# Attention and a residual MLP in one kernel: the first batch's attention in groups of four heads, mixing in column halves, PSUM in three pools, and the first MLP block by quarters of a weight

## The chip, the cores and the metric

The kernel runs on one core of one Trainium2 chip. The metric is the device time of one execution in microseconds, as the median of many runs. Engines are called as in the profile: PE is the matrix engine, PEld its weight loads, DVE the vector engine, ACT the scalar engine, POOL the GpSimd engine, and SP the engine that here only issues transfers.

## The reference, cut to what matters

```
q, k, v: (8 batches, 8 heads, 576 positions, 64)   float32
k_p, v_p = means of k, v over 8 positions each      -> 72 pooled positions
attn  = softmax(0.125 * q @ k_p^T)                  -> 576 x 72 for each head
x     = attn @ v_p, heads side by side              -> (8, 576, 512)

a1    = alpha1 * x + beta1
tok   = w_tok @ a1                                  (mixes the 576 positions of a batch)
u     = x + lam * tok
a2    = alpha2 * u + beta2
out   = u + lam * (relu(a2 @ w_ch1) @ w_ch2)        w_ch1: 512 x 2048, w_ch2: 2048 x 512
```

## The kernel before

**Tiles.** The 576 positions of a batch are four chunks of 128 and a rest of 64. Two batches put their rests together, so that two batches make nine chunks; all 36 chunks are worked through by the MLP in nine blocks of four chunks (`NBLK`). Block 0 holds chunks 0 to 3 of batch 0, block 1 those of batch 1, block 2 begins with the joint rest of batches 0 and 1.

**Attention of a batch.** `att_F` transposes q (on PE for batches 0 and 1, by a transposing transfer later), `att_Frem` the rest. `sum_k` (on POOL) and `att_K` pool k; batch 0 has no `sum_k`, and there `double_k` copies a slice instead. `att_V` pools v by three adds on DVE (batch 0: `first_V`, on PE). The scores come from `att_S4` for four heads at once: two banks `hi`, two banks `lo` and two for the rests, and twelve exponentials on ACT in two groups of six. Batch 0 uses `att_S` instead, head by head, with keys padded by zeros in `kpT_pool`. `att_AV` multiplies by v and divides on DVE (L524, L526) into `x_tm`; `att_X` and `rest_X` multiply by lam and alpha1 into `xs`.

**Mixing and MLP.** `mix_T` multiplies a chunk by w_tok (five products of 512 columns; the fifth brings the last 64 positions, beta1 and the row sums that `setup_rowsum` makes), adds x into `u_sb` and makes `u_bf = u * alpha2`. `mix_uT` brings it feature-major into `u_fm`: for block 0 by PE transposes and an ACT copy, for all others by a transposing transfer on SP's queue. `mlp_A(n, j)` makes hidden rows j of block n (j from 0 to 15) with a relu on ACT; `mlp_B(n, m, part)` multiplies them by a quarter of w_ch2 for chunk m, and after part 3 DVE scales and adds (L649, L650) and SP stores.

**PSUM.** Eight banks: `psA` has six, handed out in turn by `gp(name)`, `psB` two (tag "ch": fillers, `lo`, and `mlp_B` for chunks 0 and 1). A bank is given out again when its readers are through.

**Order.** The schedule is written by hand. Every engine executes its instructions in program order. First a straight list (L659 to L748) does batch 0's attention, its mixing, and the first four `mlp_A` in column halves, with `keep_warm` fillers for PE. Then each block n is a list of (position, action) that is sorted by position: `mlp_A` j at j, `mlp_B` at 16 + 4m + part, and in between the attention and mixing of batch n + 1 and the loads for batch n + 2. In block 0 `att_K(1, 1)` stands at 8.6, `att_S4(1, 0)` at 9.0, `att_S4(1, 1)` at 13.6 and the mixing of batch 1 from 21.0 on. A transfer waits in its queue; POOL's queue is also POOL's instruction stream, so a load is issued only when the work before it on POOL is done.

Of the kernel before, what the change touches and what calls it, by code (L numbers as in the profile page):

```python
# [23 lines left out]
def kernel(  # L24
# [24 lines left out]
    psA = ctx.enter_context(tc.tile_pool(name="psA", bufs=6, space=bass.MemoryType.PSUM))  # L49
    psB = ctx.enter_context(tc.tile_pool(name="psB", bufs=2, space=bass.MemoryType.PSUM))  # L50

    def gp(name):
        return psA.tile([P, 512], FP, tag="gp", name=name)

# [115 lines left out]
    def load_wtok():  # L170
# [4 lines left out]
        nc.gpsimd.dma_start(out=wt_bf[0:REM, 4 * S:5 * S], in_=moe_w_tok[512:576, :])  # L175

# [3 lines left out]
    b2row = const.tile([4, P], FP, tag="b2row", name="b2row")  # L180
# [18 lines left out]
    nc.scalar.dma_start(out=b2row, in_=moe_beta2.rearrange("(c p) -> c p", p=P))  # L199
# [32 lines left out]
    vp1_pool, kpT_pool, kp_pool, ET_pool = [], [], [], []  # L232
    for i in range(4):
# [3 lines left out]
        if i < 2:  # L237
            t = const.tile([P, 2, 4, SPG], BF, tag=f"kpT_{i}", name=f"kpT_{i}")
            nc.vector.memset(t, 0.0)
            kpT_pool.append(t)  # L240
            kp_pool.append(const.tile([P, 4, SPG], BF, tag=f"kp_{i}", name=f"kp_{i}"))
# [14 lines left out]
    def bias_row(i):  # L256
        p0 = 64 - 64 * i
        nc.vector.tensor_tensor(out=xs_pool[i][p0:p0 + 1, 4, :], in0=vecs[p0:p0 + 1, 1],
                                in1=vecs[p0:p0 + 1, 0], op=ALU.mult)

    b2c_bf = const.tile([P, 4], BF, tag="b2c_bf", name="b2c_bf")
    wtT = const.tile([P, 6, 640], BF, tag="wtT", name="wtT")
# [8 lines left out]
    def load_al2(behind):  # L271
        behind.memset(al2_bc[:, 0:1], 0.0)
        nc.sync.dma_start(out=al2_bc, in_=moe_alpha2.unsqueeze(0).to_broadcast((P, DM)))

    def spread_lam():

        ps = gp("ps_bc")
# [3 lines left out]
    def spread_al1(half):  # L281

        ps = gp("ps_bc")[:, 0:256]
# [4 lines left out]
    def setup_vectors():  # L288
        ps = gp("ps_vec")
        nc.tensor.transpose(out=ps[:, 0:4], in_=b2row, identity=identity[0:4, 0:4])  # L290
        nc.scalar.copy(out=b2c_bf, in_=ps[:, 0:4])

    def setup_wtok(tcx, copy):
# [4 lines left out]
        ps_w = gp("ps_w").bitcast(BF)  # L298
# [7 lines left out]
    def setup_rowsum(tcx):  # L306
# [3 lines left out]
        ps = gp("ps_rs")  # L310
# [32 lines left out]
    def setup_bias(g):  # L343
        ps_bias = gp("ps_bias")
# [8 lines left out]
    def att_F(b, hp, copy=nc.scalar.copy):  # L353
# [11 lines left out]
        ps_q = gp("ps_q").bitcast(BF)  # L365
# [30 lines left out]
    def att_K(b, u, copy):  # L396
# [21 lines left out]
        for a in range(2):  # L418
# [442 lines left out]
```

The softmax here doesn't subtract the row's maximum and nothing guards it: scores larger than these inputs give would overflow.

## Time and profile before

| what | value |
|---|---|
| median of 13 runs | 346.08 us (345.45 to 349.08) |
| the profiled execution itself | 348.03 us, span 346.3 us |
| busy in the span | PE 334.8, PEld 177.1, DVE 224.7, ACT 146.9, POOL 91.3 us |
| moved by DMA | 45.77 MB, mean 132 GB/s |
| `mlp_A` products (L609), `mlp_B` products (L643) | 132.1 us, 128.5 us |
| mixing products (L572) | 44.8 us |
| PE begins block 1 | 71.62 us |
| PE begins blocks 2 and 3 | 107.21 and 143.70 us |

A matmul of 512 columns takes 216 ns in a row of them; its own record reads about 379 ns, since its end is modelled and overlaps the next. Busy sums are averages over the whole span. The first 72 us differ from the rest: there all weights and the data of three batches are loaded, at 122 to 273 GB/s in the first eight of the forty slices.

### The profile page before, as it was taken

Reading aid. Unit: us, or ns where it says so; the run is one execution under the profiler, and the core shown is the slowest. Engines: PE = TensorE matmul, PEld = TensorE weight load, DVE = VectorE, ACT = ScalarE, POOL = GpSimd, SP = SyncE. Lnnn points to the kernel's source line nnn. Section 1 sums busy time; section 2 is a strip of 40 time slices with the busy share of each in tenths; the row PEclk is TensorE's granted clock in tenths of the full one; section 3 lists DMA queues with packets and bytes.
Section 4 is the critical chain, followed back from the end, with each engine's and each line's share of the span. In section 5 each row is a group of like instructions: output and inputs, shape, how many; then the busy total and the mean of one; then the engine's idle time right before and its main releaser. Section 6 shows DMA issues by size and latency. Waiting matters only on the chain.

```text
span 346.3 us, 5862 instructions
## 1 busy us (share of the span) xinstructions
PE 334.8 (97%) x2181; PEld 177.1 (51%) x2221; DVE 224.7 (65%) x476; ACT 146.9 (42%) x277; POOL 91.3 (26%) x105
## 2 busy tenths in 40 slices
PE   8999999979999999999999999999999999999995
PEld 3667654445544554455445544554455445545544
DVE  6674578787676668875867598758685882037511
ACT  3656980048303840286018700890079005704700
POOL 8768603601126011801180027001600100000000
PEclk9999999999999999999999999999999999999999
DMA  8999999987758925896379628991810132011012
GB/s 122 191 221 273 213 205 220 166 158 130 157 182 186 189 45 136 195 209 80 104 211 188 98 75 207 180 157 53 227 62 1 39 84 78 0 61 62 2 50 71
DMA packets 66654, 45.77 MB, mean 132 GB/s; under 512 B 34457, under 2 KB 57373, under 8 KB 66626
## 3 DMA queue, kind: packets, MB, share of 16 engines
q1 hardware_dynamic: 51716, 32.73, 41.3%
q0 software_dynamic: 14448, 12.40, 22.6%
q8 instruction: 17, 0.28, 0.3%
q10 hardware_dynamic: 462, 0.27, 0.3%
q14 instruction: 11, 0.09, 0.1%
HBM read 38.30 MB, written 9.44 MB: 138 GB/s over the span
## 4 chain that ended last, share of the span: by engine, by line
PE 82%; DMA 12%; POOL 2%; DVE 1%; issue 1%; SPq 0%; ACT 0%; DVEq 0%; POOLq 0%
PE ps_h L609 31%; PE ps_ch L643 31%; PE ps_tok L572 9%; DMA u_fm<-u_bf 5%; DMA w<-in_moe_w_ch_dram 4%; DMA rem_raw<-in_k_dram 3%; PE ps_av L518 2%; PE ps_s L474 2%; PE ps_ch L632 1%; PE ps_warm L563 1%; PE ps_kp L404 1%; POOL k_raw L162 1%; POOL k_bf L164 1%; PE ps_sc L454 1%; PE ps_bc L278 1%
## 5 line engine op out<-in xcount | busy, mean ns | idle before, releaser
L614 ACT ACTIVATE Hj<-ps_h,bias_cols 128x512 bf16<-128x512 f32 x144 | 98.3, 689 | 167.3 <-PE ps_h L609 166.0
L609 PE MATMUL ps_h<-u_fm,w 128*128 128x512 bf16 (+1 forms) x572 | 132.1, 374 | 3.3 <-DMA u_fm<-u_bf 2.0
L643 PE MATMUL ps_ch<-w,Hj 128*128 128x512 bf16 x543 | 128.5, 379 | 1.2 <-issue 0.5
L609 PEld LDWEIGHTS <-w 128*128 128x128 bf16 x592 | 63.7, 114 | 54.1 <-issue 5.7
L643 PEld LDWEIGHTS <-Hj 128*128 128x128 bf16 x560 | 52.9, 98 | 62.1 <-issue 2.1
L572 PE MATMUL ps_tok<-xs,wtT 128*128 128x512 bf16 (+2 forms) x199 | 44.8, 380 | 0.6 <-DVE xs L540 0.3
L649 DVE TENSOR_TENSOR ps_ch<-lam_bc,ps_ch 128x512 f32<-128x512 f32 x32 | 22.2, 693 | 32.8 <-PE ps_ch L643 32.5
L540 POOL TENSOR_TENSOR xs<-x_tm,lamal_bc 128x512 bf16<-128x512 f32 x10 | 12.7, 1268 | 111.2 <-DVE x_tm L526 109.5
L576 DVE TENSOR_TENSOR u_sb<-x_tm,ps_tok 128x512 f32<-128x512 f32 (+1 forms) x40 | 27.4, 684 | 10.9 <-PE ps_tok L572 10.7
L524 DVE RECIPROCAL rec<-ps_av 128x5 f32<-128x5 f32 x64 | 12.2, 191 | 32.5 <-PE ps_av L522 32.4
L526 DVE TENSOR_TENSOR x_tm<-ps_av,rec 128x320 f32<-128x320 f32 x64 | 31.5, 492 | 2.7
L650 DVE TENSOR_TENSOR u_sb<-u_sb,ps_ch 128x512 f32<-128x512 f32 x35 | 24.0, 687 | 13.6 <-PE ps_ch L643 12.5
L503 ACT ACTIVATE ET<-ps_s 72x512 f16<-72x512 f32 x56 | 32.3, 592 | 0.0
L442 DVE TENSOR_TENSOR v_u<-v_u 72x512 f32<-72x512 f32 (+1 forms) x56 | 30.9, 551 | 1.0
L579 DVE TENSOR_TENSOR u_bf<-u_sb,al_bc 128x512 bf16<-128x512 f32 x34 | 26.9, 792 | 3.5 <-DMA u_fm<-u_bf 2.4
L572 PEld LDWEIGHTS <-wtT 128*128 128x128 bf16 (+3 forms) x200 | 17.3, 100 | 21.3 <-issue 1.7
L162 POOL TENSOR_TENSOR k_raw<-k_raw 128x512 f32<-128x512 f32 x14 | 18.4, 1314 | 12.5 <-DMA k_raw<-in_k_dram 12.5
L164 POOL TENSOR_TENSOR k_bf<-k_raw 128x512 bf16<-128x512 f32 x14 | 18.4, 1317 | 1.1
L518 PEld LDWEIGHTS <-ET 72*128 72x128 f16 x256 | 14.1, 97 | 8.7 <-DVE vp L435 0.2
L79 POOL DMA_DIRECT2D q_bf<-in_q_dram x16 | 12.6, 788 | 14.6 <-DVE v_u L136 13.3
L540 DVE TENSOR_TENSOR xs<-x_tm,lamal_bc 128x512 bf16<-128x512 f32 x22 | 15.4, 702 | 0.7
L518 PE MATMUL ps_av<-vp,ET 72*128 72x66 f16 x256 | 15.8, 193 | 0.2 <-issue 0.2
(121 smaller groups left out, 214.6 us busy)
## 6 DMA issues: line engine op xcount, KB each, us to landing
out_dram<-u_sb SPq DMA_DIRECT2D x32, 256.0 KB
k_raw<-in_k_dram SPq DMA_DIRECT2D x12, 512.0 KB
v_u<-in_v_dram SPq DMA_DIRECT2D x12, 512.0 KB
q_bf<-in_q_dram POOLq DMA_DIRECT2D x16, 256.0 KB, 6.4
w<-in_moe_w_ch_dram POOLq DMA_DIRECT2D x8, 512.0 KB, 15.1
v_u<-in_v_dram POOLq DMA_DIRECT2D x2, 576.0 KB, 16.5
k_raw<-in_k_dram POOLq DMA_DIRECT2D x2, 512.0 KB, 15.5
rem_raw<-in_q_dram SPq DMA_DIRECT2D x15, 64.0 KB
```

Of the source, the lines that this page charges most:

```text
L442: nc.vector.tensor_tensor(out=t[:, :, 0:n], in0=t[:, :, 0:n], in1=t[:, :, n:2 * n], op=ALU.add)
L503: nc.scalar.activation(out=o, in_=i, func=AF.Exp, bias=0.0, scale=0.125)
L518: nc.tensor.matmul(out=av[:, odd + c, :], lhsT=ET[:, m0:m0 + 128], rhs=vp1[:, hh, :])
L526: nc.vector.tensor_tensor(out=x[:, 1 - odd:6 - odd, dd:dd + D], in0=av[:, :, 0:64], in1=rec.unsqueeze(2).to_broadcast((P, 5, D)), op=ALU.mult)
L540: eng.tensor_tensor(out=xs[:, 0:4, cols], in0=x[:, 1:5, cols], in1=lamal_bc[:, cols].unsqueeze(1).to_broadcast((P, 4, D * (h1 - h0))), op= ...
L572: nc.tensor.matmul(out=ps_tok[p0:p1], lhsT=wtT[0:kk, at, P * c:P * c + p1 - p0], rhs=xs_pool[i][0:kk, sc, :], start=(sc == 0), stop=(sc == 4))
L576: nc.vector.tensor_tensor(out=s["u"][p0:p1, :], in0=x[p0:p1, 1 + c if c < 4 else 5 - 5 * i, :], in1=ps_tok[p0:p1, 0:DM], op=ALU.add)
L579: eng.tensor_tensor(out=s["u_bf"], in0=s["u"], in1=al2_bc, op=ALU.mult)
L609: nc.tensor.matmul(out=ps_h[:, t0:t1], lhsT=w1_of(cc, j), rhs=u_fm[n][:, cc, t0:t1], start=(cc == 0), stop=(cc == 3))
L614: nc.scalar.activation(out=t, in_=ps_h, func=AF.Relu, bias=bias_cols[:, j:j + 1], scale=1.0)
L643: nc.tensor.matmul(out=ps, lhsT=Hj[n, j][:, 128 * m:128 * m + 128], rhs=w2[j // 4][:, j % 4, :], start=(j == 0), stop=(j == NJ - 1))
L650: nc.vector.tensor_tensor(out=u, in0=u, in1=ps, op=ALU.add)
```

## The change

- Batch 0 takes its scores by `att_S4` too; `att_S` and `kpT_pool` go. The list of the front is put in a new order: heads 2 and 3 first, `setup_vectors` earlier, twelve fillers instead of sixteen.
- Mixing of batch 0 is done in column halves: `mix_half` multiplies by the first four row groups for 256 columns (four heads), and `mix_T` adds the fifth product at the end.
- Chunks 1 and 3 of block 0 have no `u_bf`: `mix_uT_fp` transposes `u_sb` itself in fp32 and multiplies by alpha2, held as columns in `al2c`, on the way out of PSUM.
- Batch 1's chunks are transposed on PE, as batch 0's were, and no longer by a transfer.
- PSUM: `psA` four banks, `psB` two, and a new `psX` with two (`xp`), which takes `hi`, heads 2 and 3 of `att_AV`, `mlp_B` for chunks 2 and 3, and work of the front.
- Block 0 does parts 0 and 1 of `mlp_B` for all four chunks, then parts 2 and 3 chunk by chunk.
- Loads: alpha2's rows go to POOL's queue in the front; batch 1's k is issued after batch 0's last `att_X`; batch 1's v in two halves, each after a quarter of w_ch1, and all of these after the mixing's `u_bf` products. In block 0 some positions move (`att_V`, heads 0 to 3 of `att_AV`, mixing 21.5 instead of 21.0).

```diff
-    psA = ctx.enter_context(tc.tile_pool(name="psA", bufs=6, space=bass.MemoryType.PSUM))
+    psA = ctx.enter_context(tc.tile_pool(name="psA", bufs=4, space=bass.MemoryType.PSUM))
     psB = ctx.enter_context(tc.tile_pool(name="psB", bufs=2, space=bass.MemoryType.PSUM))
+    psX = ctx.enter_context(tc.tile_pool(name="psX", bufs=2, space=bass.MemoryType.PSUM))
+    def bp(name):
+        return psB.tile([P, 512], FP, tag="ch", name=name)
+    def xp(name):
+        return psX.tile([P, 512], FP, tag="hi", name=name)
...
# load_wtok
+        nc.gpsimd.dma_start(out=al2_bc, in_=moe_alpha2.unsqueeze(0).to_broadcast((P, DM)))
...
-    nc.scalar.dma_start(out=b2row, in_=moe_beta2.rearrange("(c p) -> c p", p=P))
+    nc.scalar.dma_start(out=b2row[0:4], in_=moe_beta2.rearrange("(c p) -> c p", p=P))
+    nc.scalar.dma_start(out=b2row[4:8], in_=moe_alpha2.rearrange("(c p) -> c p", p=P))
...
# setup_vectors
-        nc.tensor.transpose(out=ps[:, 0:4], in_=b2row, identity=identity[0:4, 0:4])
+        nc.tensor.transpose(out=ps[:, 0:8], in_=b2row, identity=identity[0:8, 0:8])
         nc.scalar.copy(out=b2c_bf, in_=ps[:, 0:4])
+        nc.scalar.copy(out=al2c, in_=ps[:, 4:8])
...
# att_K, batch 0
-        for a in range(2):
-            rows = slice(64 * a, 64 * a + 64)
-            (copy or (nc.scalar.copy, nc.vector.tensor_copy)[a])(
-                out=kpT_pool[u][rows, a], in_=kp[rows])
+        for i, eng in ((2, nc.scalar.copy), (0, nc.scalar.copy if u else nc.vector.tensor_copy)):
+            eng(out=kp_pool[u][:, i:i + 2], in_=kp[:, i:i + 2])
...
# att_S4
-        lo = [psB.tile([P, DM], FP, tag="ch", bufs=2, name="ps_s") for _ in range(2)]
-        hi = [gp("ps_s") for _ in range(2)]
-        r = [gp("ps_r")[0:SPG, 0:128].rearrange("p (h i) -> p h i", i=64) for _ in range(2)]
+        lo = [(bp if b else gp)("ps_s") for _ in range(2)]
+        hi = [xp("ps_s") for _ in range(2)]
+        r = [(gp if b else bp)("ps_r")[0:SPG, 0:128].rearrange("p (h i) -> p h i", i=64)
+             for _ in range(2)]
...
# att_AV
-        ps_av = gp("ps_av")
+        ps_av = (xp if b and h in (2, 3) else gp)("ps_av")
...
+    def mix_half(c, half):
+        if half == 0:
+            ps_mix[c] = gp("ps_tok")
+        cols = slice(256 * half, 256 * half + 256)
+        for sc in range(4):
+            nc.tensor.matmul(out=ps_mix[c][:, cols], lhsT=wtT[:, sc, P * c:P * c + P],
+                             rhs=xs_pool[0][:, sc, cols], start=(sc + half == 0), stop=False)
...
# mix_T
-        for sc in range(5):
+        first = b == 0 and c < 4
+        ps_tok = ps_mix[c] if first else gp("ps_tok")
+        for sc in range(4 if first else 0, 5):
...
+        if eng is not None:
+            eng.tensor_tensor(out=s["u_bf"], in0=s["u"], in1=al2_bc, op=ALU.mult)
+
+    def mix_uT_fp(c):
+        ps = xp("ps_uT")
+        if 0 not in u_fm:
+            u_fm[0] = work.tile([P, 4, 512], BF, tag="u_fm", bufs=3, name="u_fm")
+        for cc in range(4):
+            nc.tensor.transpose(out=ps[:, 128 * cc:128 * cc + 128],
+                                in_=st2[0, c]["u"][:, 128 * cc:128 * cc + 128], identity=identity)
+        for cc in range(4):
+            nc.vector.tensor_scalar(out=u_fm[0][:, cc, 128 * c:128 * c + 128],
+                                    in0=ps[:, 128 * cc:128 * cc + 128],
+                                    scalar1=al2c[:, cc:cc + 1], scalar2=None, op0=ALU.mult)
...
# mix_uT
-        if blk:
+        if key[0] > 1 or key == (0, 4):
             nc.sync.dma_start_transpose(out=u_fm[blk][:, :, 128 * at:128 * at + 128],
...
# the list of the front, as it is after the change
+    load_q_bf(1, 0)
+    bias_row(0, nc.gpsimd)
+    load_q_bf(1, 1)
...
+    att_Frem(0, nc.scalar.copy)
+    setup_vectors()
+    keep_warm(1)
+    double_k(0)
+    att_K(0, 0, None)
+    keep_warm(1)
+    def scores(u):
+        att_S4(0, u)
+        for k in range(6):
+            st1[0]["exp", u](k)
+    scores(0)
+    double_k(1)
+    first_V(0, 0)
+    att_K(0, 1, None)
+    att_AV(0, 2)
+    att_F(0, 2, bank=xp)
+    att_F(0, 3, nc.vector.tensor_copy, xp)
+    att_AV(0, 3)
+    spread_al1(0)
+    att_X(0, 2, 4, nc.gpsimd, False)
+    att_AV(0, 0)
+    keep_warm(1)
+    scores(1)
+    first_V(0, 1)
+    att_AV(0, 1)
+    att_X(0, 0, 2, nc.gpsimd, False)
+    rest_X(0, 0, 4, nc.gpsimd)
+    keep_warm(1)
+    att_AV(0, 4)
+    spread_al1(1)
+    att_AV(0, 5)
+    load_rem(1, behind=nc.vector)
+    att_X(0, 4, 6, nc.gpsimd, False)
+    keep_warm(1)
+    setup_wtok(0, nc.scalar.copy, xp)
+    setup_wtok(1, nc.scalar.copy, xp)
+    att_AV(0, 6)
+    att_AV(0, 7)
+    att_X(0, 6, 8, rest=False)
+    rest_X(0, 4, 8)
+    for u in range(2):
+        load_k(1, u, queue=nc.gpsimd)
+    setup_wtok(2, nc.scalar.copy, bp)
+    setup_wtok(3, nc.scalar.copy, bp)
+    mix_half(0, 0)
+    setup_rowsum(0)
+    mix_half(1, 0)
+    setup_rowsum(1)
+    mix_half(2, 0)
+    mix_half(0, 1)
+    setup_rowsum(2)
+    mix_T(0, 0, nc.gpsimd)
+    mix_half(3, 0)
+    setup_rowsum(3)
+    mix_half(1, 1)
+    mix_T(0, 1, None)
+    mix_half(2, 1)
+    mix_T(0, 2, nc.gpsimd)
+    mix_half(3, 1)
+    mix_T(0, 3, None)
+    load_w1(2)
+    load_v(1, 0, (2,), queue=nc.gpsimd)
+    load_w1(3)
+    load_v(1, 1, (2,), queue=nc.gpsimd)
+    for g in range(2):
+        load_w2(g)
+    setup_bias(0, bp)
+    mix_uT_fp(1)
+    mix_uT((0, 0))
+    setup_wtok(4, nc.scalar.copy, bp)
+    setup_bias(1, bp)
+    mlp_A(0, 0, 0, 256)
+    mix_uT((0, 2))
+    mix_uT_fp(3)
+    for j in range(1, 4):
+        mlp_A(0, j, 0, 256)
+    for j in range(4):
+        mlp_A(0, j, 256, 512)
...
# attention(b): positions in block 0
-            at = 26.6 if first else 25.5
+            at = 27.5 if first else 25.5
...
-            for i, dt in enumerate((2.9, 3.4, 4.6, 5.1) if u else (5.7, 6.2, 2.9, 3.4)):
+            late = ((5.7, 6.2, 4.0, 4.5), (2.9, 3.4, 4.6, 5.1))[u]
+            for i, dt in enumerate(late if first else (2.9, 3.4, 4.6, 5.1) if u else (5.7, 6.2, 2.9, 3.4)):
...
-            todo.append(((6.6, 8.7, 10.0, 12.6)[i] if first else 0.2 + 2.0 * hp, lambda hp=hp: att_V(b, hp)))
+            todo.append(((9.5, 9.6, 11.6, 11.7)[i] if first else 0.2 + 2.0 * hp, lambda hp=hp: att_V(b, hp)))
...
-            at = 21.0 + 1.3 * c
+            at = (21.5 if first else 21.0) + 1.3 * c
...
-                todo.append((at + 1.8, lambda key=key: mix_uT(key)))
+                todo.append((at + (2.6 if first and c < 4 else 1.8), lambda key=key: mix_uT(key)))
...
# the blocks
-                at = 16 + 4 * m + part
+                at = 16 + (4 * part + m if n == 0 and part < 2 else 4 * m + part)
+                if n == 0 and part > 1:
+                    at = 24 + 2 * m + part - 2
...
-                    at = (14.51 if b == 1 else 21.0) + 0.01 * u
+                    at = (15.01 if b == 1 else 21.0) + 0.01 * u
```

## The prediction

> **What bounds the kernel now.** I read the page first: PE is busy for 334.8 of 346.3 us, so a change pays only where it removes PE work from the end-setting order or closes a PE gap. Next the chain of waits, for where it leaves PE:
>
> ```profile
> 22.36 9.08 DMA rem_raw<-in_k_dram
> ...
> 38.00 14.76 DMA w<-in_moe_w_ch_dram
> 52.80 2.75 PE ps_ch L643 x12
> ...
> 58.11 13.37 DMA u_fm<-u_bf x2
> 71.62 4.48 PE ps_h L609 x20
> ```
>
> Up to 71.6 us the chain runs through transfers, afterwards almost only through PE. Block 1 begins at 71.62; everything behind it (274.7 us) is PE in a fixed order. So I ask one thing: when does block 1 begin? The PE timeline gives its gaps, 0.24, 0.34 and 1.81 us:
>
> ```profile
> 31.78 1.91 PE L609 MATMUL ps_h<-u_fm,w 128*128 128x256 bf16 x16 [0.24 <-ACT u_fm L595]
> ...
> 47.03 1.06 PE L609 MATMUL ps_h<-u_fm,w 128*128 128x512 bf16 x4
> ...
> 52.80 2.75 PE L643 MATMUL ps_ch<-w,Hj 128*128 128x512 bf16 x12 [0.34 <-DMA w<-in_moe_w_ch_dram]
> ...
> 71.62 3.62 PE L609 MATMUL ps_h<-u_fm,w 128*128 128x512 bf16 x16 [1.81 <-DMA u_fm<-u_bf]
> ```
>
> The reader is to see that only the last one is worth a change of its own.
>
> The table of stretches shows DMA occupied without a break (a share over 1 in every stretch from 20 to 66 us). How long POOL's loads then take from issue, the views by line and by tile tell; first w_ch1's last quarter (issued at 26.2), then v_u, batch 1's v in two halves (issued at 22.5 and 23.2):
>
> ```profile
> DMA to landing us min/median/max: 16.7/16.7/16.7
> ```
> ```profile
> L139 POOL DMA_DIRECT2D v_u<-in_v_dram x2: 728/741/754, 22.5 to 23.2; - x2
> ...
> DMA to landing us min/median/max: 15.2/16.5/17.8
> ```
>
> So v_u's halves land at 22.5+15.2=37.7 and 23.2+17.8=41.0, w_ch1's last quarter at 26.2+16.7=42.9. This is a queue worked off in order: what is put ahead arrives first, what is put behind arrives later. Last the timeline of DVE, for three rows that the sum needs: the att_X that ends the front, two of the three adds of an att_V, and a u_bf product beside POOL's sum_k, which takes 1.62 where 0.69 is usual:
>
> ```profile
> 22.08 0.69 DVE L540 TENSOR_TENSOR xs<-x_tm,lamal_bc 128x512 bf16<-128x512 f32 x1
> ...
> 41.80 1.14 DVE L442 TENSOR_TENSOR v_u<-v_u 72x512 f32<-72x512 f32 x2
> ...
> 61.99 1.62 DVE L579 TENSOR_TENSOR u_bf<-u_sb,al_bc 128x512 bf16<-128x512 f32 x1
> ```
>
> **The front (to the fifth mlp_A).** Scores: 16 ACT exps (0.70 a head, 5.6) become 12 (as in block 0: 0.44 for two, then 0.49 each, 4.8); PE 8x0.30 becomes 2x0.72, -0.96; four fillers go, -0.86. kpT's memsets (-0.6 DVE, early) and half-row copies (0.39/0.46) become 144-column copies (0.27/0.31 by their slope). k16's second half lands at 6.06+5.8=11.9 as now, and double_k(1) now stands ahead of first_V on DVE: ready 12.15. From 13.1 (att_K 0.72 and an AV on PE first) DVE has eight AVs x0.70, a qT copy and two alpha1 products x0.41, 0.49, 0.06 and att_X 0.69: 8.1, done at 21.2 against 22.75. DVE, not PE, sets this stage: take DVE's cover away and the PE savings above would show; as it is they only lengthen PE's waits. Halves cost no extra columns (eight of 0.108 and a tail of 0.216 against five of 0.216), and more weight loads hide, as under mlp_A's 256-column halves now (16 in 1.74 us). PE has by then three column halves of mixing (3x0.43) behind it. From 21.2: the other five halves 2.16, four tails 0.86, two row sums 0.56, to 24.85; two bias groups 1.10, a bf16 transpose 0.22, wtok 0.28, fp32 transposes 0.53, to 27.0; then mlp_A 3.46, 0.22, 0.53: 31.35 instead of 33.52, **2.2 earlier**. Two u_bf (1.38) and two ACT copies (1.18) become eight DVE products (about 0.25 each from the 72x128 row's 0.29, 2.0), the first four under bias and wtok, the last under mlp_A. bias_row moves from DVE (0.68) to POOL, whose wait for k16 covers it (0.5 idle plus 0.9); rest_X is halved (0.43 DVE, 0.87 POOL); al2c's copy is 0.15 ACT; the second b2row load costs 0.25 of ACT's queue, and setup_vectors at 7.9 waits for it (bounds 0 and 1 us: its twin was issued at 3.96; I take 0, since k16 lands only at 8.1 anyway).
>
> *The fp32 transposes.* No 128x128 one is in the trace. The nearest fp32 rows are b2row's transpose (weight load 133 ns, one pass) and the broadcast product (0.62 for 256 columns in two passes). The first gives 4x0.133=0.53 a chunk, the second 1.24. [...] I take 0.53; the other end costs 1.4 more, and is covered as shown below.
>
> **Loads and queues.** al2_bc goes from SP to POOL's queue ahead of w_ch1 (0.57 of POOL); same bytes, landed by 25 both ways. The two k_raw leave 13.8/15.5 for about 20.7, behind att_X on POOL; the queue holds work to 28.2 then, so they still land near 29.4 and 30.8. w_ch1(2) to w_ch2(1) now stand behind both u_bf products on POOL: u_bf done at 26.4, six issues 4.2, 30.6; cast_rem 1.1, sum_k 2.6, an issue 0.58, sum_k 2.55: k_bf(1) at 37.5 against 38.0. PE, 2.2 early, wants it at 37.5: no wait. And v_u's second half now follows w_ch1(3): it lands at 42.9, not 41.0. SP's queue loses al2_bc (0.35) and four u_fm transposes (1.2 to 2.0 each), which brings batch 2's qT transposes forward, not back. Batch 2's k, v and rem loads go from position 14.5 to 15.0: their seven gating memsets (0.6 of DVE) come behind AV 0's evacuation, at about 49.4 instead of 48.4; sum_k(2) then ends near 68 instead of 67, and PE asks for it at 75: nothing.
>
> **Block 0, first half.** That is the cost. DVE executes att_V(2), att_V(3) at 42.9 or later (2x1.38), and only then AV 2 and 3 (0.70+0.63): 47.03. Those AVs now take psX's two banks, which att_S4(1,1) needs for hi. PE would be there at about 44.4 and stands for some 2.5 us; after it 0.06, 0.11+0.08+0.22: att_S4 ends at **47.45, before it was 47.03**. So the 2.2 of the front is spent, with 0.4 more. The same slack takes in the fp32 bound (+1.4, u_fm later) and waits on gp, four banks instead of six, while ACT lags by up to 1.1 us on a stretch where it is busy 4.5 of 5 us (bounds 0 and 0.8). [...]
>
> **Block 0, second half.** From the fifteenth mlp_A to the block's end it was 69.81-47.03=22.78. The order by quarters needs w_ch2's third and last quarter at positions 24 and 25, about 58 us, against landings of 50.3 and 52.8: -0.34. Four PE transposes of batch 1's u: +0.88, with ACT copies on an idle ACT. The gap of 1.81 goes, since u_fm no longer queues behind batch 2's k and v. Late next is DVE: all four output evacuations (1.39 each) fall into the last 8 us, with 1.4 a chunk for u. By my sum chunk 3's u_bf is ready 2.2 us before its transpose and DVE ends 1.5 us after PE; three u_bf beside POOL's sum_k at +0.93 would be 2.8 more. That is covered until batch 2's kp copy (PE wants it 6.5 us into block 1; I get 4.6 to 7.3): bounds 0 and 0.8, taken 0, the case without overlap being the nearer row (two of five u_bf overlapped before).
>
> Block 1 begins at 47.45+22.44+0.88=70.77 instead of 71.62: **-0.85**. Later blocks: mlp_A 7 reuses the bank of mlp_A 6, whose relu ends at 150.88 where PE comes at 150.93; taken 0, bounds 0 and 0.1 a block. The gap of 0.22 at block 2 stays. The profiled execution (346.3 span, 1.73 around it, 348.03, which is 1.95 above the median of 13) would be 345.45 and 347.2; the median 346.08-0.85=**345.2**.
>
> **Rivals.**
> *A, the sum above (0.42).* Its own range is 344.4 to 346.0, for a landing 0.8 us either way. 0.3% of the time is 1.04 us, about what a measurement of this kernel can tell from no change; A straddles it, half and half.
> *B, the front's gain survives (0.32).* If v_u's second half lands by 41.4, DVE is the limit: 41.4+2.76+1.33+0.42=45.9, block 1 at 69.2: -2.4, 343.7. For it: v_u's 0.59 MB took 3.3 to 3.6 us where w_ch1(3) behind it took only 1.9, so the two overlap in the queue, and one may slip past the other. Against: the order of landing was so far the order of issue.
> *C, the load queue runs dry (0.21), slower.* w_ch1(2) used to be issued at 21.7; it now waits for the second u_bf. k_raw is through at 30.8, and the shortest issue to landing in this trace is 4.8 us, of it about 3.5 latency, so from an issue at 27.3 on every microsecond is one of idle DMA and one later for v_u, att_S4(1,1) and the end. I have 26.4: a margin of 0.9. At 29.8 (the front gains nothing and loses 0.8) v_u lands at 45.4, block 1 begins at 73.3: 347.7. For it: the front is a long sum. Against: DVE's stretch is nearly gapless and made of measured rows.
> *D, the closed gap comes back (0.05).* If DVE lags, PE stands at chunk 3's transpose for what DMA cost before (-0.93 lost): 346.1.
>
> Faster: B and half of A, 0.52; same: half of A and D, 0.27; slower: C, 0.21. The range 343.2 to 347.6 reaches to B and C at their worked prices and leaves out about 0.1 on each side: B with a stage that runs under its sum, C with an issue after 29.8 or with the dearer ends of the unknown costs added to it.
>
> **What would show it.** Right: mlp_A's fifth near 31.4; PE waiting 2 to 3 us at ps_s near 45 for DVE's x_tm, DVE before it for v_u; no wait for w or u_fm in block 0; block 1 at 70.8. An fp32 transpose row near 0.13 and not 0.3. Wrong: no wait at that ps_s (B), w_ch1(2) issued after 28 (C), or PE waiting on kp or ps_uT behind DVE near 68 to 76.

## The result, and the profile after

The changed kernel takes **349.99 us** (median of 11 runs, 347.48 to 355.95) against 346.27 for the kernel before in the same comparison: ratio 1.0096, 95% interval 1.0077 to 1.0115, so 1% slower. Forecast were 345.2 and a range of 343.2 to 347.6. Ratios compare only executions that lie within 1.5% of the fastest of their kernel; the medians quoted are of more executions, so that a few long ones can lift a median above what its ratio says.

The profiled execution took 348.22 us with a span of 346.5. First its PE timeline in the places where the prediction had put something. Columns: start, duration, engine, line, operation, shapes, count, and in brackets the idle time before and what ended it.

```profile
9.28 0.24 PE L293 MATMUL ps_vec<-identity,b2row 8*128 8x8 f32 x1 [0.75 <-DMA b2row<-in_moe_alpha_dram]
9.46 0.61 PE L554 MATMUL ps_warm<-warm 128*128 128x512 bf16 x1
...
12.58 1.07 PE L432 MATMUL ps_v<-v,pool_v 128*72 128x256 f16 x4
...
27.98 0.63 PE L591 MATMUL ps_uT<-identity,u_sb 128*128 128x128 f32 x4
28.45 0.39 PE L610 MATMUL ps_uT<-identity_bf,u_bf 128*128 128x128 bf16 x4
...
33.76 0.65 PE L371 MATMUL ps_q<-identity_bf,q_bf 128*128 128x128 bf16 x8
34.61 1.03 PE L626 MATMUL ps_h<-u_fm,w 128*128 128x512 bf16 x3 [0.20 <-ACT Hj L631]
...
47.91 0.30 PE L461 MATMUL ps_s<-qT,kp 64*72 64x256 bf16 x1 [0.33 <-DVE x_tm L517]
...
48.53 0.30 PE L461 MATMUL ps_s<-qT,kp 64*72 64x256 bf16 x1 [0.33 <-DVE x_tm L517]
...
71.96 2.32 PE L626 MATMUL ps_h<-u_fm,w 128*128 128x512 bf16 x10
```

The reader is to see five things. PE waits 0.75 us for the second row load of b2row, a place that had no wait before. The filler behind it takes 0.61 us, where the fillers at 18.87 and 20.18 of the same profile take 0.38; the four products of first_V take 1.07, where those of its second call, at 17.81, take 0.63. Four fp32 transposes begin 0.47 us ahead of the next group: 0.12 each. The front's first four mlp_A are through at 33.76, where PE turns to q's transposes, and the fifth begins at 34.61, not near 31.4. Block 1 begins at 71.96 without a wait for u_fm, but it is not earlier.

At ps_s, near 48, PE waits only 0.33 us twice, since it comes there late itself. DVE, too, is late there by PE's lateness: it copies kp when PE has done att_K(1,1), and only then starts the four att_V, which run without a gap up to the evacuations that free psX:

```profile
41.07 0.46 DVE L420 CAST kp<-ps_kp 128x288 bf16<-128x288 f32 x1 [2.15 <-PE ps_kp L414]
```

In the chain of waits, which in the kernel before ran here through PE and the copies out of PSUM, now stands the new load:

```profile
4.24 4.79 DMA b2row<-in_moe_alpha_dram
```

It is issued at 4.24 on ACT's queue and is there at 4.24+4.79=9.03. Last the table of stretches. Its columns: the stretch and its length, busy time and count of PE, PEld, DVE, ACT and POOL, then the granted clock, the DMA share and GB/s.

```profile
28.00:30.00 2.00, 2.00 (x37) 1.83 (x35) 1.46 (x5) 1.23 (x4) 2.00 (x3) 1.00 0.59 198
30.00:32.00 2.00, 2.00 (x22) 1.99 (x21) 1.09 (x5) 0.59 (x1) 2.00 (x3) 1.00 0.73 92
32.00:34.00 2.00, 2.00 (x22) 1.99 (x21) 0.63 (x2) 1.29 (x3) 2.00 (x5) 1.00 1.24 214
```

DMA is less than fully busy from 28 to 32 (a share of 0.59 and 0.73), since POOL issues w_ch1(2) only at 28.98. This is the picture of rival C; whether it is also the price had to be tried.

### The profile page after: what moved, and what is told of

Its sections match the earlier page's. It is cut to its first block, busy times and chain, and to the rows that moved or that the text cites. A ratio compares the mean times of both kernels' runs of the same rounds, so it can differ in the third digit from the quotient of the medians.

```text
span 346.5 us, 5909 instructions
## 1 busy us (share of the span) xinstructions
PE 336.2 (97%) x2210; PEld 179.5 (52%) x2249; DVE 222.9 (64%) x477; ACT 147.2 (42%) x277; POOL 92.9 (27%) x108
## 4 chain that ended last, share of the span: by engine, by line
PE 90%; DVE 4%; ACT 2%; DMA 1%; issue 1%; ACTq 1%; DVEq 0%
PE ps_ch L660 34%; PE ps_h L626 33%; PE ps_tok L575 11%; PE ps_s L461 2%; PE ps_av L509 2%; DVE v_u L444 2%; DMA b2row<-in_moe_alpha_dram 1%; ACT Hj L631 1%; PE ps_tok L564 1%; PE ps_ch L649 1%; PE ps_kp L408 1%; PE ps_r L468 1%; DVE x_tm L517 1%; PE ps_av L513 1%; PE ps_bias L352 0%
## 5 line engine op out<-in xcount | busy, mean ns | idle before, releaser
L575 PE MATMUL ps_tok<-xs,wtT 128*128 128x512 bf16 (+3 forms) x183 | 41.4, 380 | 0.3
L494 ACT ACTIVATE ET<-ps_s 72x512 f16<-72x512 f32 x64 | 36.4, 593 | 0.0
L579 DVE TENSOR_TENSOR u_sb<-x_tm,ps_tok 128x512 f32<-128x512 f32 (+1 forms) x40 | 27.3, 684 | 11.5 <-PE ps_tok L575 11.4
L583 DVE TENSOR_TENSOR u_bf<-u_sb,al_bc 128x512 bf16<-128x512 f32 x32 | 25.6, 799 | 2.2 <-DMA u_fm<-u_bf 1.2
L575 PEld LDWEIGHTS <-wtT 128*128 128x128 bf16 (+3 forms) x184 | 16.0, 100 | 19.3 <-issue 1.9
L169 POOL TENSOR_TENSOR k_raw<-k_raw 128x512 f32<-128x512 f32 x14 | 19.2, 1368 | 11.4 <-DMA k_raw<-in_k_dram 11.4
```

The source lines that it names most:

```text
L494: nc.scalar.activation(out=o, in_=i, func=AF.Exp, bias=0.0, scale=0.125)
L575: nc.tensor.matmul(out=ps_tok[p0:p1], lhsT=wtT[0:kk, at, P * c:P * c + p1 - p0], rhs=xs_pool[i][0:kk, sc, :], start=(sc == 0), stop=(sc == 4))
L579: nc.vector.tensor_tensor(out=s["u"][p0:p1, :], in0=x[p0:p1, 1 + c if c < 4 else 5 - 5 * i, :], in1=ps_tok[p0:p1, 0:DM], op=ALU.add)
L583: eng.tensor_tensor(out=s["u_bf"], in0=s["u"], in1=al2_bc, op=ALU.mult)
```

## The experiments

In front of each expectation stands the edit; where nothing else is said it is against the changed kernel. "Half-clock executions" are those with a mean granted clock of 0.995 or less. That is 0.005 of some 346 us, or 1.7 us of clock lost, as much as 3.4 us at half clock (0.50, the lowest reading in the tables of stretches). The slow matmuls at the start do not enter it: there the granted clock reads 1.00 (in the changed kernel in each stretch from 6 to 16). The kernel before has 6 of them in the 149 executions of it that enter the ratios of these experiments. Counts like "3 of 8" are of executions that enter the ratio.

**The changed kernel again.** No edit.

> The changed kernel once more, for a second profile and a time on the same chip as the three others. In its first profile TensorE came to full clock at 14.0 us of the span, in that of before at 8.3. If the lost time lies in this (theory T1: PE's new wait of 0.75 us for b2row's second row, and the half clock that lasts longer for it), the profile shows full clock late again, or lost a second time before 20 us, and the time is 2 to 4 us above before, about 349 to 350. If it lies in the order of the front and in block 0 (theory T2: VectorE's chain up to att_S4(1,1), which ended at 48.95 instead of 47.03), the span goes with the end of that att_S4 and not with the clock.

352.44 (349.14 to 355.54; three of the six took 354.5 or more), ratio 1.0090 [1.0069, 1.0111]. The ratio rests on the other three, 349.14 to 350.34, and none of them is a half-clock execution: most of the loss is there without half clock. The wait for b2row was 2.00 us in its profile (350.34 us), w_ch1(2) left at 30.26, and block 1 began at 74.08.

```profile
10.18 0.24 PE L293 MATMUL ps_vec<-identity,b2row 8*128 8x8 f32 x1 [2.00 <-DMA b2row<-in_moe_alpha_dram]
```

**setup_vectors back where it was.**

```
-    setup_vectors()            # behind att_Frem(0)
+    setup_vectors()            # ahead of att_AV(0, 4)
```

> One line moved: setup_vectors goes from the place after att_Frem to the place ahead of att_AV(0, 4), where before had it. T1: no wait for b2row at 9.3 us, att_K(0,0) begins near 8.5 instead of 9.9, full clock by about 9 us, and the time falls by 2 to 5 us, to 345 to 347.5, the prediction's 345.2 being the front without that wait. T2: PE's wait only moves elsewhere, and the time stays within 1 us of the changed kernel's (349 to 350).

348.73, ratio 1.0059 [1.0040, 1.0079]. In the profile (346.74 us, span 345.0) the wait is gone and the filler takes 0.38 us at 8.11:

```profile
8.11 0.38 PE L554 MATMUL ps_warm<-warm 128*128 128x512 bf16 x1
...
31.42 0.65 PE L371 MATMUL ps_q<-identity_bf,q_bf 128*128 128x128 bf16 x8
...
46.42 0.30 PE L461 MATMUL ps_s<-qT,kp 64*72 64x256 bf16 x1 [1.19 <-DVE x_tm L517]
...
47.05 0.30 PE L461 MATMUL ps_s<-qT,kp 64*72 64x256 bf16 x1 [0.33 <-DVE x_tm L517]
...
47.47 1.06 PE L626 MATMUL ps_h<-u_fm,w 128*128 128x512 bf16 x4
...
70.47 0.81 PE L626 MATMUL ps_h<-u_fm,w 128*128 128x512 bf16 x3
```

DVE, ahead of those two evacuations, waits for v_u's second half:

```profile
42.82 1.14 DVE L444 TENSOR_TENSOR v_u<-v_u 72x512 f32<-72x512 f32 x2 [0.96 <-DMA v_u<-in_v_dram]
```

With this one line moved the chain of the prediction is there: v_u at 42.8 (forecast 42.9), att_S4(1,1) ended at 47.47 (47.45), block 1 at 70.47 (70.77). And yet the median is above the kernel before. Three of 8 executions are half-clock ones (median 349.3); the other five have a median of 347.5.

**Two fillers ahead of the early setup_vectors.**

```
+    keep_warm(2)
     setup_vectors()            # behind att_Frem(0)
```

> The changed kernel with two more fillers ahead of setup_vectors, so that PE is busy while it waits for b2row; the wait itself stays. T1 with the clock as the larger part: full clock by about 9 to 10 us though att_K(0,0) still begins at about 9.9; the time falls by 1.5 to 4 us, to about 346 to 348. T1 with the wait itself as the larger part, or T2: no gain, 349 to 350.5.

349.96, ratio 1.0098 [1.0073, 1.0123]: no better than the changed kernel, although the profile shows only 0.24 us of wait there, and the filler behind it, at 9.17, takes 0.39 us instead of 0.61 in the changed kernel. Four of 6 executions are half-clock ones, and the profile is one. The stretches around att_S4(1,1):

```profile
46.00:48.00 2.00, 0.30 (x1) 0.11 (x1) 1.79 (x7) 0.00 (x0) 0.00 (x0) 1.00 1.05 211
48.00:50.00 2.00, 1.79 (x15) 1.15 (x16) 1.14 (x3) 1.10 (x4) 0.00 (x0) 0.86 1.14 210
50.00:52.00 2.00, 2.00 (x11) 0.87 (x9) 0.89 (x9) 1.19 (x3) 0.00 (x0) 0.50 1.13 184
52.00:54.00 2.00, 1.95 (x12) 0.84 (x11) 1.81 (x5) 1.45 (x3) 0.00 (x0) 0.78 0.93 144
```

PE is busy for 0.30 of the 2 us from 46 on (waits of 1.78 and 0.33 us for DVE's x_tm); the granted clock then falls to 0.50, and PE gets through 11 matmuls in a full stretch, where it gets through 19 at this place of the program in the profile with setup_vectors late. In the last row, at 0.78, the clock comes back. The loss is 2 x (0.14+0.50+0.22) = 1.7 us of clock, so 3.4 us at half clock.

**The kernel before with setup_vectors early.** b2row with 8 rows, its second load, the al2c copy, and setup_vectors behind att_Frem(0); nothing else of the change.

> The kernel before with this one part of the change: b2row of eight rows, the second load on ACT's queue, setup_vectors after att_Frem, and al2c's copy (al2c is not used). T1: PE waits for b2row near 8 to 9.3 us, the clock comes late or goes back, and the time rises by 1.5 to 4 us, to 347.6 to 350. T2: the wait is covered by batch 0's k, which lands at 8.1, and the time stays within 0.5 us of before (345.6 to 346.8).

347.84, ratio 1.0044 [1.0027, 1.0061]: 1.5 us dearer than the kernel before, with a wait of 0.76 us in the profile:

```profile
8.81 0.24 PE L292 MATMUL ps_vec<-identity,b2row 8*128 8x8 f32 x1 [0.76 <-DMA b2row<-in_moe_alpha_dram]
```

So this part alone is a loss of 0.9 to 2.1 us by the interval. In the profile block 1 begins at 70.73, 1.5 us later than in a profile of the kernel before without this part (69.22, below), twice the wait that is seen: matmuls at the start stay slow for longer as well (the filler behind the wait takes 0.61 us and the next one, at 10.39, still 0.59, against 0.38 at 8.94 in the kernel before). Half-clock executions: none of 8.

**att_V(2) and att_V(3) behind AV 2 and 3**, once with setup_vectors late and once without.

```
-  (9.5, 9.6, 11.6, 11.7)[i]
+  (9.5, 9.6, 13.55, 13.56)[i]
```

> The changed kernel with setup_vectors put back to ahead of att_AV(0,4) and, in addition, att_V(2) and att_V(3) of batch 1 executed by DVE behind the evacuations of AV 2 and 3 (positions 11.6, 11.7 become 13.55, 13.56). Theory (the starved stretch ahead of att_S4(1,1) costs its own 1.5 us and, in about half of the executions, 3.4 us of half clock behind it): PE no longer waits at ps_s for DVE's x_tm near 45; AV 2 and 3 are evacuated as soon as they are done, near 44; att_S4(1,1) ends near 46, block 1 begins near 69, no execution shows a clock of 0.993, and the median is 344.5 to 346, at or below the kernel before. Rival 1 (the wait only moves: v_u's second half still lands at 42.8 and AV 4 and 5 wait for att_V(2) instead): att_S4(1,1) ends early but PE waits at AV 4 or at the following mlp_A, block 1 at 70.3 or later, median near 347. Rival 2 (the half clock comes from something else than that stretch): 0.993 in about as many executions as with setup_vectors alone put back (3 of 8), median near 348.

> The changed kernel with only the two att_V of batch 1 moved behind the evacuations of AV 2 and 3; setup_vectors stays early, and with it the wait for alpha2's row. If the two causes are separate and add up: the front is as in the changed kernel (wait for b2row of 0.7 to 2 us, full clock from 12 to 16 us, fifth mlp_A near 34.6 or later), no wait at ps_s near 45, no clock of 0.993; about 1.5 to 2.5 us below the changed kernel, 347.5 to 348.5, still above the kernel before. If the stretch at att_S4(1,1) is not what costs: no change, 350.

The first: 348.18, ratio 1.0059 [1.0038, 1.0081]; the second: 349.12, 1.0070 [1.0052, 1.0088]. Half-clock executions fall to 2 of 20 (from 3 of 8) and 1 of 15 (from 7 of 11), so the order at that stretch bears on the clock. The wait, though, only moved, as the first rival said of the kind, if not of the place; in the first one:

```profile
46.64 1.05 PE L626 MATMUL ps_h<-u_fm,w 128*128 128x512 bf16 x4
...
56.37 1.24 PE L575 MATMUL ps_tok<-xs,wtT 128*128 128x512 bf16 x5 [1.56 <-DVE xs L531]
```

att_S4(1,1) ends 0.8 earlier, DVE is later with everything behind, and PE waits 1.56 us at the mixing (1.56 in the second run too). This wait is as long as the one it replaces (1.19 and 0.33), and the clock behind it reads 1.00 in the first profile (from 56 to 58); the mean clock of the second is 0.998. So the length of a wait alone does not decide on the half clock: behind 1.38 us it came (the first run with 256 KB less, below).

**AV 2 and 3 in gp** (with setup_vectors late).

```
-  (xp if b and h in (2, 3) else gp)
+  (xp if b > 1 and h in (2, 3) else gp)
```

> As with setup_vectors put back, and batch 1's AV 2 and 3 take gp instead of psX, so that att_S4(1,1) finds psX free however late DVE is. If it is the tie of psX to DVE's order that starves PE: the wait at ps_s goes and block 1 begins 1 us or more earlier than 70.47. If four banks of gp are what is short: the wait reappears at the next users of gp (the rest scores, AV 0 and 1, mlp_A), of the same size, and block 1 stays at 70.3 to 70.8; the theory leans to this, since gp's banks come round every fourth request and DVE is as late as before.

347.67, ratio 1.0021 [1.0000, 1.0042], half-clock executions 4 of 19. The wait reappears at the rest scores, so the four banks and DVE's order bind here too:

```profile
46.70 0.26 PE L468 MATMUL ps_r<-rem_qT,kp 64*72 64x64 bf16 x1 [1.32 <-DVE x_tm L517]
```

By its ratio it is the best variant of the changed kernel, and still not below the kernel before.

**The kernel before, profiled twice more.** No edit.

> The kernel before, profiled once more. The profile that the prediction used is of an execution 1.95 us above the median. If its wait of 1.81 us for u_fm ahead of block 1 belongs to every execution, it is here again at 1.5 or more and block 1 begins near 71.6. If it is what made that execution long: the wait is under 0.6 here, block 1 begins near 70, the span is near 344.5, and the gain of 1.81 that the prediction booked for closing it was in the median only to a small part.

> The kernel before, profiled again. An execution near the median (346.3, span 344.5) should begin block 1 near 69.8, without a wait for u_fm of over 0.5 us; if it begins at 71.6 with the wait of 1.81, the time must be 348.

The first execution was a half-clock one (349.07 us): from 16 to 22 its clock was 0.50 to 0.56, and block 1 began at 73.06, but without any wait for u_fm. The second took 345.45 us, 0.8 below the median:

```profile
64.89 4.49 PE L643 MATMUL ps_ch<-w,Hj 128*128 128x512 bf16 x20
69.22 4.48 PE L609 MATMUL ps_h<-u_fm,w 128*128 128x512 bf16 x20
```

Block 1 begins at 69.22 and there is no wait in front of it. The 1.81 us on which the prediction rested are in one of three profiles, the one it read. There POOL got batch 2's k_raw late:

```profile
60.45 1.27 POOL L162 TENSOR_TENSOR k_raw<-k_raw 128x512 f32<-128x512 f32 x1 [3.77 <-DMA k_raw<-in_k_dram]
```

In both later profiles it comes without a wait. That the late landing is what made u_fm late is argued, not tried.

**The kernel before with batch 1's transposes on PE.**

```
-        if blk:
+        if key[0] > 1 or key == (0, 4):        # else PE transposes, at +2.6
```

> The kernel before with one part of the change alone: batch 1's four u_fm chunks are transposed on PE (at the change's positions) instead of by SP's DMA queue. The prediction's booking: the wait of 1.81 us for u_fm ahead of block 1 goes, four transposes cost 0.88, so 0.93 faster, 345.3 (ratio 0.997). The other theory: that wait belongs to the one profiled execution and not to the median one, so only the cost is left, 0.88 slower, 347.1 (ratio 1.0025).

347.49, ratio 1.0038 [1.0025, 1.0051]. The booking of the prediction (0.997) is out; the cost without the gain (1.0025) lies at the edge of the interval. In the profile block 1 begins 23.01 us behind the end of att_S4(1,1) (70.68-47.67), in the profile of 345.45 us 22.12 (69.22-47.10): 0.89, where 0.88 was forecast.

**v_u's second half ahead of w_ch1's last quarter** (setup_vectors late), and then also batch 1's u_fm on SP's queue again.

```
     load_v(1, 0, (2,), queue=nc.gpsimd)
-    load_w1(3)
     load_v(1, 1, (2,), queue=nc.gpsimd)
+    load_w1(3)
```

> As with setup_vectors put back, and the second half of batch 1's v issued ahead of w_ch1's last quarter, as in the kernel before. If the landing of v_u at 42.8 sets DVE's att_V(2), att_V(3), and these the release of psX: v_u lands near 41, the wait at ps_s falls from 1.5 to 0.3 us or less, att_S4(1,1) ends near 46, block 1 begins near 69, hardly an execution at clock 0.993, and the median is 345.5 to 346.5, level with the kernel before or better. Rival (DVE is late by its own work, not by the landing): the wait stays over 1 us, 348. Second rival: w_ch1's last quarter is now late and PE waits for w at mlp_A 12 near 44.

> As the run before it, with batch 1's four u_fm chunks also put back on SP's DMA queue. If the wait for u_fm belongs to few executions: 0.9 us below the run before it, 344.8 to 345.6, faster than the kernel before by up to 0.4%. If block 1's earlier start makes the DMA transposes late: a wait for u_fm ahead of block 1 of 0.9 us or more, and no gain over the run before it.

The first: 347.45, ratio 1.0027 [1.0015, 1.0040], no half-clock execution in 22. DVE does not wait for v_u any more, but the quarter is late, as the second rival said:

```profile
43.87 0.70 PE L352 MATMUL ps_bias<-b2c_bf,w 128*128 128x1 bf16 x16 [1.10 <-DMA w<-in_moe_w_ch_dram]
```

The second: 350.56, ratio 1.0109 [1.0076, 1.0142]. Here u_fm is truly late, by 2.77 us:

```profile
73.35 6.17 PE L626 MATMUL ps_h<-u_fm,w 128*128 128x512 bf16 x20 [2.77 <-DMA u_fm<-u_bf]
...
74.00:76.00 2.00, 2.00 (x6) 0.74 (x5) 1.66 (x5) 0.69 (x1) 0.00 (x0) 0.50 1.35 73
```

SP issues the last of these transposes at 70.78, behind an output store that it holds until 70.37, while DVE had the chunk's u_bf done at 68.9. The order by quarters brings the stores of block 0 into its last 8 us, so in this profile it is the change itself that makes the queue late, and the PE transposes are what it needs. And the 20 matmuls take 6.17 us instead of 4.48: the granted clock is 0.50 from 74 to 76, as the second row, of the table of stretches, shows.

**Loads issued ahead of POOL's u_bf products** (setup_vectors late).

```
     load_k(1, u, queue=nc.gpsimd)
+    load_w1(2); load_v(1, 0, ...); load_w1(3); load_v(1, 1, ...)
```

> As with setup_vectors put back, and the four loads w_ch1(2), v_u, w_ch1(3), v_u leave POOL ahead of its two u_bf products instead of behind them (near 22.3 to 25.4 instead of 26.6 to 29.7). If the issue sets the landing: v_u lands up to 1 us or more earlier than 42.8 and the wait at ps_s (1.5) falls by as much, 347. If the queue's volume sets it (in the run with setup_vectors put back the table of stretches shows no dry stretch from 20 to 46): v_u lands at 42.3 to 42.8 as before, and POOL's later u_bf costs PE up to 1.2 us at the transposes of chunks 0 and 2, which the wait at ps_s takes in: 348.7 again.

348.02, ratio 1.0057 [1.0037, 1.0077]. The issues move from 26.6 to 22.8, and DVE no longer waits for v_u; but PE waits 0.42 for POOL's u_bf, the fifth mlp_A goes from 32.27 to 33.39, and att_S4(1,1) ends at 47.64, 0.17 later than with setup_vectors alone put back. What DVE waits for now is PE's att_K(1,1), which is late with the front:

```profile
39.78 0.46 DVE L420 CAST kp<-ps_kp 128x288 bf16<-128x288 f32 x1 [2.08 <-PE ps_kp L414]
...
46.60 0.30 PE L461 MATMUL ps_s<-qT,kp 64*72 64x256 bf16 x1 [0.23 <-DVE x_tm L517]
47.22 0.30 PE L461 MATMUL ps_s<-qT,kp 64*72 64x256 bf16 x1 [0.33 <-DVE x_tm L517]
```

With setup_vectors alone put back this copy stands at 38.66. If the early issue had left the front alone, att_S4(1,1) would have ended near 38.66+7.86=46.5 by these rows; that is an estimate and was not tried. The landing itself did not come forward: v_u's second half, issued at 25.1 instead of 28.9, landed at 43.0 (25.1+17.9) instead of 42.8.

Half-clock executions: 9 of 21, the most of all variants with 15 executions or more, though the profile (a full-clock execution) shows waits of only 0.23 and 0.33 us at ps_s and 0.42 at u_bf. The profiles do not show where the half clock comes from here.

**256 KB less in the load queue.** al2_bc is spread on PE from a row of 2 KB instead of loaded; the two products took the place of two fillers in the first pair, which differs by the order of v_u and w_ch1(3). In the second pair the fillers were kept and the loads issued early.

> As with setup_vectors put back, and al2_bc no longer comes as a load of 256 KB in POOL's queue ahead of w_ch1: a row of 2 KB is loaded on ACT's queue and spread by two products on PE in the place of two fillers, and two ACT copies. Theory (the load queue's volume up to v_u's second half sets att_S4(1,1)): at the 210 to 230 GB/s of the table of stretches 256 KB are 1.1 to 1.2 us, so v_u lands near 41.6 instead of 42.8, the wait at ps_s falls from 1.5 to about 0.4 us, att_S4(1,1) ends near 46.4, block 1 begins near 69.4, executions at clock 0.993 become rare, median 346 to 346.8. Rival (the landing hangs on when POOL issues, behind the u_bf products, and not on the volume): v_u lands at 42.5 or later and nothing changes, 348.7.

> The same saving of 256 KB, and v_u's second half issued ahead of w_ch1's last quarter. By the volume theory both the wait for w near 43.8 (1.10 with the load) and the wait at ps_s go: block 1 near 69.3 to 70, median 346 to 346.6, level with the kernel before, since the four PE transposes of batch 1 (0.9) stay. By the rival the wait for w stays at about 1 us, 347.4.

> The early issue together with the row of 2 KB in the place of al2_bc's 256 KB, with both fillers kept. If the fillers' absence caused the half clock from 20.3 to 23.7 in the run without them: full clock through the front, fifth mlp_A near 33. With an early issue and 256 KB less, v_u lands near 41.5 by the volume theory: the wait at ps_s 0.3 to 0.6 us, block 1 near 69.6 to 70, median 346.2 to 347. If the two products themselves (one row of weights) let the clock fall: half clock again near 20, 350 or more.

> The same with v_u's second half ahead of w_ch1's last quarter. By the volume theory neither ps_s nor w is waited for by more than 0.4 us, block 1 near 69.5 to 70, median 346 to 346.8. If w's last quarter is still late, PE waits for w near 44 by up to 1 us, 347.5.

353.29, 351.12, 350.57 and 348.98; ratios 1.0184 [1.0146, 1.0223], 1.0150 [1.0098, 1.0202], 1.0078 [1.0046, 1.0111] and 1.0072 [1.0048, 1.0096]. Half-clock executions: 6 of 6, 4 of 5, 2 of 4 and 4 of 5. The times do not answer the question about the volume, because the clock falls in the front. The stretches of the first:

```profile
18.00:20.00 2.00, 1.85 (x15) 1.14 (x16) 1.61 (x6) 0.45 (x4) 1.88 (x2) 1.00 1.24 204
20.00:22.00 2.00, 2.00 (x29) 1.95 (x27) 1.24 (x4) 1.92 (x4) 1.99 (x2) 0.58 1.29 204
22.00:24.00 2.00, 2.00 (x16) 1.65 (x14) 1.06 (x3) 1.05 (x3) 0.78 (x2) 0.57 1.43 201
...
28.00:30.00 2.00, 2.00 (x37) 1.72 (x35) 1.62 (x4) 0.52 (x2) 1.46 (x2) 1.00 0.14 43
```

The late front delays POOL's issues to 29.8, the queue moves only 43 GB/s from 28 to 30 (17 in the next 2 us), and v_u lands at 46.1. With both fillers kept, in the third, the clock was half from 19 to 25 all the same (0.72, 0.50, 0.50 and 0.57 in the stretches from 18 to 26), so the missing fillers are not what it takes. That the fp32 products with one row of weights are what lets the clock fall was not tried by itself; no run shows it. The added products cannot be all of it: in its half-clock profile the kernel before has the same fall from 16 on, and it has only the alpha1 products of this kind there.

On the volume, one landing says something: with both fillers kept and 256 KB less, v_u's second half was issued at 24.8 and landed at 43.0 (24.8+18.2), as it did with the 256 KB (43.0). The volume theory had 41.5. It is one profile each.

## Why the prediction was wrong, point by point

**The term that failed: "The gap of 1.81 goes, since u_fm no longer queues behind batch 2's k and v".** Block 1 did begin without a wait for u_fm, but the median execution of the kernel before has no such wait either: two later profiles show none, and closing it alone, in the kernel before, made that kernel slower. The prediction saw that its profile lay 1.95 us above the median of 13, and nevertheless carried the difference of two block-1 starts (70.77 against 71.62) over to the median unchanged. Without the gap the old start is 71.62-1.81 = 69.81, and the same sum says +0.96 instead of -0.85: 346.27+0.96 = 347.2. The executions with setup_vectors late and no half clock have a median of 347.5. The profile with setup_vectors late and the later one of the kernel before both lie 0.7 to 0.8 us below these medians, and their block-1 starts, 70.47 and 69.22, differ by 1.25. The PE transposes alone, in the kernel before, cost 1.3 us, so that they account for all that the chain loses. The sign of the forecast hung on this term.

**The second: setup_vectors, "bounds 0 and 1 us ... I take 0".** Measured were waits of 0.75 and 2.00 us in the changed kernel's two profiles (0.21 in that of the variant with only the att_V moved), and 1.5 us in the median when only this is done. The cover named, "k16 lands only at 8.1 anyway", ends too soon: where PE does not wait for the row, att_K begins at 8.1 to 8.3, and the row, the last load on ACT's queue, came at 9.0 and in the second profile at about 9.9 (an estimate: PE starts on it at 10.18, and in the first it started 0.25 after the landing). In addition PE had little to do in that stretch (busy for 1.25 of the 2 us from 8 on, and for 0.18 in the second profile), and its matmuls stay slow for 4 us or more longer: first_V's four take 1.07 us at 12.58, where with setup_vectors late they take 0.63 at 10.43, and the filler already 0.38 at 8.11. Neither bound nor sum had the slow matmuls in it.

**The third: the clock behind PE's wait at ps_s, which the sum has at nothing.** No run shows a wait of some 2.5 us with full clock behind it. The profile of the kernel before shows it for 1.81 us: the 20 matmuls behind that wait take 4.48 us, 216 ns each in the row, and the granted clock is 1.00 in each stretch from 72 to 78. In three profiles half clock follows waits of PE: 1.78 and 0.33 us (two fillers), 1.38 and 0.33 (the first with 256 KB less) and 2.77 (u_fm back on SP's queue), each time with 1.7 us of clock lost, which is 3.4 us at half clock. In two profiles it does not follow 1.19 and 0.33. So it was a risk that the sum had at nothing. How often it comes does not go by the length of the wait alone, as the runs with 1.56 us at the mixing and the run with the early loads show. The price, in the changed kernel's first comparison: the 7 of 11 executions with half clock have a median of 350.4, the other four 348.4. That is 2.0 us, near the 1.7 us of clock lost in each of the three profiles.

As an estimate from medians, the three make up the result: 346.3, plus 1.2 for what the chain itself costs (347.5), plus 0.9 for setup_vectors (348.4, full-clock executions of the changed kernel), plus 1.6 because most of its executions have the half clock (349.99). The split is not firm: in the second comparison three executions without half clock took 349.1 to 350.3, and the profile there, of the longest of these (350.34 us), has 2.00 us of wait for the row instead of 0.75.

**What was right.** fp32 transposes: 0.12 each, so 0.47 a chunk against 0.53 taken and 1.24 as the other end. v_u's landing, DVE's att_V ahead of the AV evacuations, psX held, PE standing at ps_s: all came in the variant with setup_vectors late, the times to 0.3 us, but the wait is 1.5 us (1.19+0.33) and not 2.5. In the changed kernel itself v_u does not bind in the first profile; PE's own lateness does. The four PE transposes: 0.89 against 0.88. The second half of block 0: 23.00 (70.47-47.47) against 22.44+0.88 = 23.32. No wait for w or u_fm in block 0, no wait on kp. The front: with setup_vectors late att_X ends at 21.3 against 21.2, and the first four mlp_A are through at 31.42 against 31.35. The prediction calls that point the fifth mlp_A, but the 33.52 that it compares with is the same point in the kernel before, where PE turns to q's transposes:

```profile
33.52 0.61 PE L367 MATMUL ps_q<-identity_bf,q_bf 128*128 128x128 bf16 x8
```

So the front's forecast holds to 0.07 us once the row is not waited for, although the working to it adds up to only 31.1 to 31.2 from the 21.2. The fifth mlp_A itself begins at 33.97 in the kernel before and at 32.27 with setup_vectors late.

**The rivals.** B did not come: in no run did PE get through att_S4(1,1) early and keep the gain. Its bound, 45.9, counted DVE only from v_u's landing; in the run with the early issue DVE starts its four att_V behind PE's att_K(1,1), at 40.2, and that binds (47.64). C was there as a picture (issue at 28.98, beyond its point of 27.3, a queue with idle time) but in the first profile not as the price: DVE never waits for v_u there (0.89 us in the second profile). With setup_vectors late the issue is at 26.64 and the queue stays busy from 28 to 32, and the kernel is still slower than before. It named the slower side with a time (347.7) that the real causes passed. Its 3.5 us of latency stand in no row; they are an estimate, the 4.8 us less some 1.3 for 256 KB at about 200 GB/s (194 to 214 in the stretches from 14 to 22). D did not come: PE has no wait at the transposes of batch 1's u.

What stays open: why the half clock follows in some executions and not in others with the same waits, and where it comes from in the run with the early loads; and what sets v_u's landing, which neither the earlier issue nor 256 KB less brought forward.

## What to carry to other kernels

Before a wait is booked as gain, ask whether the median execution has it: if the profiled run lies above the median by about the size of the wait, subtract the wait first, or take a second profile. A small load moved onto the critical start has to be counted from its issue (4.79 us for 2 KB here), and here PE's matmuls stayed slow for longer behind the wait as well (1.07 us for first_V's four at 12.58, instead of 0.63). And do not trade a stage bound by loads and one engine's order for savings on another engine: each of the four ways tried to free PE at att_S4(1,1) brought the wait back at ps_r, at w, at xs or at u_bf.

## What the runs showed of the hardware that was not expected

- Half clock followed some waits of PE and not others of like length: it came after 1.78 and 0.33 us (clock 0.50 from 50 to 52, with two fillers), after 1.38 and 0.33 us (0.50 from 52 to 54, the first with 256 KB less) and after 2.77 us (0.50 from 74 to 76). After 1.81 us in the kernel before the clock stayed at 1.00 (72 to 78), after 1.56 us at the mixing too (56 to 58).
- The clock lost adds up to 1.7 us in the profile with two fillers, that is 3.4 us at half clock. The first profile with 256 KB less has the same in its front (2 x (0.42+0.43) = 1.7), and the half-clock profile of the kernel before twice as much (2 x (0.44+0.50+0.50+0.26) = 3.4, so 6.8 us at half clock).
- In the front of the first profile with 256 KB less it fell to 0.58 (20 to 22) with PE busy for 1.85 of 2 us in the stretch ahead of it, where the longest wait is 0.30 us.
- At the start a wait of 0.75 us goes with matmuls that are still slow 3 us later (1.07 instead of 0.63 for the same four, at 12.58). The granted clock reads 1.00 in each stretch from 6 to 16, so there the durations show the speed and the clock column does not.
- One kernel, unchanged, shows block 1 at 69.2, 71.6 and 73.1 us in three profiles, by a late transfer in one and half clock in another.
